# Mixer's second MLP layer with 7 block products in place of 8 for four of six pairs of token tiles

## The chip, the cores and the metric

The kernel runs on one core of a Trainium2 chip. The metric is the device time of one execution in microseconds; the time before is the median of three timed runs. The engines are TensorE (PE; its weight loads are PEld), VectorE (DVE), ScalarE (ACT), GpSimd (POOL) and SyncE (SP, which issues DMAs). Each runs its own instructions in the order of the program and waits on semaphores for the others.

## What is computed

Three stages follow each other: an attention with a delta-rule state, a mixture of experts in which one expert is chosen for each token, and a Mixer. The change lies in the Mixer's MLP (two batches of 768 tokens, 384 features, 1536 hidden):

```python
def _moe2_ref(x, w_ch1, w_ch2):
    X = np.fft.fft(np.fft.fft(x, axis=1), axis=2)
    u = x + np.real(X)
    mu = np.mean(u, axis=-1, keepdims=True)
    var = np.mean((u - mu) ** 2, axis=-1, keepdims=True)
    un = (u - mu) / np.sqrt(var + 1e-06)
    ch = np.maximum(un @ w_ch1, 0.0) @ w_ch2
    return u + ch
```

## The kernel before

The Mixer works on 12 token tiles of 128 tokens, six per batch. **Front of a batch:** sums and differences of mirrored rows (`d`, `e`, from `xa`; L1127 and L1130) are split in two fp16 parts (`zh` on ACT L1190, `zl` on DVE L1192); PE multiplies them with the tables of the Fourier transform along the tokens (`yp` L1208), ACT and DVE split the result (`Y` L1263, L1265), PE transforms along the features (`fp` L1239), and DVE makes `m` (L1251, L1252), which is added to `ur`, the tile `u` (L1127). Then the statistics of the layer norm (`bs`, `ag`, `vs`, L1282 to L1299), `un` on ACT (L1304), three transposes on PE (`up` L1320) and the two fp16 parts of the transposed tile, `uT` (L1325, L1327). The first tiles are ready before the second batch's front begins, so the MLP of the first runs between pieces of the front of the second.

**MLP.** Tiles go through in groups, `GROUPS=(2, 4, 4, 2)`. Layer 1 (`mlp1`) computes, for each of 12 blocks of 128 hidden features, nine matmuls into one PSUM tile `mp`: three slices of the features times three products of the fp16 high and low parts, the weights stationary, `uT` (256 or 512 tokens wide) moving. `relu` writes the high part `mh` (ACT) and the low part `ml` (DVE). Layer 2 (`mlp2`) takes `mh` and `ml` as the stationary operand, 128 x 128, and 384 columns of `w_ch2` as the moving one, three products per tile and block, summed over the 12 blocks in one PSUM bank per tile (`mop`). `finish` adds the bank to `ur` on DVE and sends the tile out, from SP or, for two tiles of a batch, with an indirect DMA on POOL.

**Order.** Nothing of this is in the order of the source. Each piece is a Python generator that yields what it needs (an engine for so many ns, a buffer, a flag), and `Order` plays them against a clock of its own and records each instruction when its engine is granted. `MP` holds the priority of each generator, `EB` a bias in ns between DVE and POOL for the sums and differences (`eng`, `tt`), and the resources (`h`, `o`, `mh`, `uT`) are counts of buffers. So a number in a table moves instructions on every engine. Flags hold only in this plan: on the chip an instruction waits for the semaphores of the data that it reads and writes. `n01` is the flag for the second tile of the first group, transposed.

Of the kernel before, what the change touches and what calls it, by code (L numbers as in the profile page):

```python
# [728 lines left out]
class Rest:  # L729
# [657 lines left out]
    def mlp2(s):
        nc=s.nc
        for g,m in enumerate(s.GROUPS):
            yield f"H{g}0"  # L1390
            for _ in range(m): yield ("+","o")
            pm=[s.ps.tile([128,512],F32,tag="o",name="mop",bufs=4)[:,0:384] for _ in range(m)]
            for f in range(12):
                yield f"H{g}{f}"
                hs=s.hs.pop((g,f))
                for t in range(m):
                    if t==0 or f==11: yield ("T",490*m if f<11 else 490,0)
                    for n,(a,b) in enumerate(((0,0),(1,0),(0,1))):
                        nc.tensor.matmul(out=pm[t],lhsT=hs[a][:,128*t:128*t+128],rhs=s.w_ch2(b,f),start=(f==0 and n==0),stop=(f==11 and n==2))  # L1399
                    if f==11: s.add_("F",s.finish(g,t,pm[t]))  # L1400
# [127 lines left out]
```

## Time and profile before

| | us |
|---|---|
| timed runs, median (lowest to highest) | 582.86 (581.4 to 585.84) |
| profiled execution | 580.74 |
| its span | 578.9 |
| PE busy | 470.7 |
| DVE busy | 421.7 |
| ACT busy | 322.8 |
| POOL busy | 78.9 |

The mean granted clock of TensorE over the span was 0.909. Attention takes the first 245 us, the experts 250 to 394, the Mixer the rest; the first matmul of the MLP starts at 415.60 us. The rows that are quoted below are from this execution, and their times start with its span. A start and a length are given for each instruction; since instructions on an engine overlap, a pace is read from starts. Square brackets behind a row hold the idle time ahead of it and what ended it.

### The profile page before, as it was taken

How to read it: one execution, taken by the hardware profiler on the slowest of the kernel's cores; microseconds unless marked ns; L12 is line 12 of the kernel's file. 1: busy time of each engine (PE TensorE's matmuls, PEld its weight loads, DVE VectorE, ACT ScalarE, POOL GpSimd, SP SyncE). 2: the span in 40 equal slices, each digit the busy share in tenths (PEclk: the TensorE clock that was granted, in tenths of full speed). 3: DMA queues.
4: the chain of work that ended last, by engine and by line, in shares of the span. 5: the costliest groups of instructions: out<-in, count | busy, mean ns of one | idle time of the engine just before them, and what ended most of it. 6: DMA issues, size and time to landing. Idle time of an engine off the chain costs nothing.

```text
span 578.9 us, 12899 instructions
## 1 busy us (share of the span) xinstructions
PE 470.7 (81%) x5162; PEld 375.0 (65%) x5162; DVE 421.7 (73%) x943; ACT 322.8 (56%) x729; POOL 78.9 (14%) x85
## 2 busy tenths in 40 slices
PE   0642027894689799679999999999899999999997
PEld 0531017783689698568888888788787655555575
DVE  7969989898998877469888979878987643231132
ACT  3664347898698888716766766672554332111111
POOL 6000000000000000040343332125111210000010
PEclk9965556999599789879999999999999999999999
DMA  7274125186005103839999997328100000010011
GB/s 250 50 130 121 37 49 63 63 141 156 1 3 103 29 3 100 299 99 336 388 319 316 361 305 238 118 63 274 56 1 1 28 2 0 1 55 0 1 42 41
DMA packets 66991, 67.23 MB, mean 116 GB/s; under 512 B 40086, under 2 KB 59483, under 8 KB 66928
## 3 DMA queue, kind: packets, MB, share of 16 engines
q1 hardware_dynamic: 63936, 57.59, 33.5%
q0 software_dynamic: 2992, 8.79, 4.9%
q8 instruction: 41, 0.67, 0.5%
q14 instruction: 22, 0.18, 0.1%
HBM read 51.95 MB, written 7.67 MB: 103 GB/s over the span
## 4 chain that ended last, share of the span: by engine, by line
PE 27%; issue 18%; POOL 5%; DVE 3%; DMA 1%; ACT 1%; POOLq 0%; SPq 0%; ACTq 0%; DVEq 0%
PE mp L1373 12%; PE mop L1399 12%; POOL xg L901 3%; POOL x2d L939 2%; PE fp L1239 1%; PE yp L1208 1%; DMA xa<-x2d 1%; PE up L1320 1%; DVE zl L1192 0%; DMA x2d<-ot,sim 0%; ACT zh L1190 0%; DVE e L1127 0%; DVE Y L1265 0%; DVE ws L894 0%; DVE d L1127 0%
## 5 line engine op out<-in xcount | busy, mean ns | idle before, releaser
L1383 DVE SCALAR_TENSOR_TENSOR ml<-mp,mh 128x256 f16<-128x256 f32 (+1 forms) x48 | 26.8, 558 | 81.0 <-ACT mh L1381 80.9
L1373 PE MATMUL mp<-uT,ws 128*128 128x256 f16 (+1 forms) x432 | 77.8, 326 | 0.0
L1399 PE MATMUL mop<-ws,mh 128*128 128x384 f16 x288 | 77.7, 326 | 0.0
L1381 ACT ACTIVATE mh<-mp 128x256 f16<-128x256 f32 (+1 forms) x48 | 23.5, 489 | 89.8 <-PE mp L1373 89.6
L930 PE MATMUL op<-ws,hh 128*128 128x384 f16 (+1 forms) x256 | 67.5, 326 | 0.0
L918 PE MATMUL hp<-xT,ws 128*128 128x240 f16 x576 | 64.6, 266 | 0.9 <-DVE xT L909 0.5
L312 PEld LDWEIGHTS <-KT 128*128 128x128 f16 x576 | 27.5, 118 | 51.6 <-issue 40.1
L918 PEld LDWEIGHTS <-ws 128*128 128x128 f16 x576 | 56.2, 98 | 6.9 <-issue 1.3
L1373 PEld LDWEIGHTS <-ws 128*128 128x128 f16 x432 | 42.2, 98 | 27.2
L894 DVE SCALAR_TENSOR_TENSOR ws<-raw,ws 128x1536 f16<-128x1536 f32 x32 | 55.9, 1749 | 0.0
L312 PE MATMUL ga<-ST,KT 128*128 128x64 f16 x288 | 16.2, 224 | 42.2 <-DVE ST L308 37.7
L891 ACT ACTIVATE ws<-raw 128x1536 f16<-128x1536 f32 x32 | 47.3, 1485 | 0.7 <-DMA raw<-moe_w 0.7
L1399 PE MATMUL mop<-ws,ml 128*128 128x384 f16 x144 | 46.9, 326 | 0.0
L930 PE MATMUL op<-ws,hl 128*112 128x384 f16 (+1 forms) x128 | 41.7, 326 | 0.0
L1399 PEld LDWEIGHTS <-mh 128*128 128x128 f16 x288 | 28.2, 98 | 17.8
L901 POOL DMA_INDIRECT xg<-xd,gm x16 | 23.0, 1437 | 117.4 <-DVE fl L1063 110.0
L930 PEld LDWEIGHTS <-hh 128*128 128x128 f16 (+1 forms) x256 | 29.1, 114 | 11.6
L373 DVE TENSOR_TENSOR P<-P,tmp 128x31 f32<-128x31 f32 (+15 forms) x93 | 31.5, 338 | 1.7
L371 DVE TENSOR_TENSOR tmp<-Gu,P 128x31 f32<-128x31 f32 (+15 forms) x93 | 31.2, 336 | 1.6
L921 DVE SCALAR_TENSOR_TENSOR hl<-hp,hh 128x480 f16<-128x480 f32 x32 | 20.9, 654 | 14.5 <-ACT hh L920 12.9
L939 POOL DMA_INDIRECT x2d<-ot,sim x16 | 19.3, 1204 | 86.9 <-ACT ot L935 84.4
L920 ACT ACTIVATE hh<-hp 128x480 f16<-128x480 f32 x32 | 18.1, 567 | 20.7 <-PE hp L918 19.5
(274 smaller groups left out, 1176.9 us busy)
## 6 DMA issues: line engine op xcount, KB each, us to landing
raw<-moe_w SPq DMA_DIRECT2D x64, 384.0 KB
x<-moe_w_ch SPq DMA_DIRECT2D x24, 384.0 KB
qp<-q SPq DMA_DIRECT2D x5, 512.0 KB
kp<-k SPq DMA_DIRECT2D x6, 384.0 KB
vp<-v SPq DMA_DIRECT2D x6, 384.0 KB
xd<-yb SPq DMA_DIRECT2D x48, 48.0 KB
xa<-x2d SPq DMA_DIRECT2D x6, 384.0 KB
ur<-x2d SPq DMA_DIRECT2D x2, 768.0 KB
```

The costliest lines, as they stand in the source:

```text
L312: s.nc.tensor.matmul(out=out,lhsT=st[l],rhs=mv[m],start=(first and i==0),stop=True,skip_group_check=True)
L371: nc.vector.tensor_tensor(out=x,in0=Gu[:,k,k+1:32].unsqueeze(2).to_broadcast([128,m,n]),in1=P[:,k,0:n].unsqueeze(1).to_broadcast([128,m,n] ...
L373: nc.vector.tensor_tensor(out=P[:,k+1:32,0:n],in0=P[:,k+1:32,0:n],in1=x,op=ALU.subtract)
L891: s.nc.scalar.activation(out=s.W[q][:,0].rearrange("p s c -> p (s c)"),in_=s.raw[q],func=AF.Copy,scale=WS)
L894: s.nc.vector.scalar_tensor_tensor(out=W[1],in0=s.raw[q],scalar=WS,in1=W[0],op0=ALU.mult,op1=ALU.subtract)
L901: nc.gpsimd.indirect_dma_start(out=s.xg[e][t][0:w],out_offset=None,in_=s.xd,in_offset=bass.IndirectOffsetOnAxis(ap=s.gi[0:w,8*t+e:8*t+e+1] ...
L918: nc.tensor.matmul(out=p[:,i],lhsT=s.W[q][:,a,i,128*k:128*k+128],rhs=xT[b][:,k],start=(n==0),stop=(n==8)); n+=1
L930: nc.tensor.matmul(out=s.po[t][0:w],lhsT=hs[a][:,i,128*t:128*t+w],rhs=s.W[q][:,b,i,384:768],start=(g==0 and i==0 and n==0),stop=(g==3 and ...
L939: i=s.nc.gpsimd.indirect_dma_start(out=s.x2d,out_offset=bass.IndirectOffsetOnAxis(ap=s.si[0:w,c:c+1],axis=0),in_=ot,in_offset=None,bounds_ ...
L1373: for k in range(3): nc.tensor.matmul(out=p,lhsT=s.w_ch1(a,k,f),rhs=s.uT[g][b][:,k,0:N],start=(n==0),stop=(n==8)); n+=1
L1383: nc.vector.scalar_tensor_tensor(out=hl,in0=p,scalar=0.0,in1=hh,op0=ALU.max,op1=ALU.subtract)
L1399: nc.tensor.matmul(out=pm[t],lhsT=hs[a][:,128*t:128*t+128],rhs=s.w_ch2(b,f),start=(f==0 and n==0),stop=(f==11 and n==2))
```

## The change

The groups become six pairs of tiles. For pairs 1 to 4 (`STR`), layer 2 is computed as a product of 2 x 2 blocks with seven block products (Winograd's form of Strassen's). The blocks are: two token tiles, two halves of the hidden features (block j and block j+6), two halves of the 384 output columns.

- **Layer 1** makes, for each j of 6, two `mp` of 256 tokens. For the seven products their ReLU goes to fp32 (`zz`, ACT), four 128 x 128 sums follow on DVE or POOL (`C` in `EB`), and `pair` splits three and then four of the blocks in `mh` and `ml` (ACT copy, DVE subtraction, both from SBUF).
- **Layer 2** (`seven`): for each j seven products of three matmuls with 192 columns, into four banks; `first4` and `last3` put the seven sums together, with additions on DVE or POOL.
- **The weights' sums** (`combine`): twelve sums of 128 x 2 x 192 in fp32, six ACT copies and six DVE subtractions of 128 x 2 x 384, in place in the tiles that held the raw weights (`dec`), which now stay to the end. In the plan they begin with `n01`.
- `uT` is 256 wide with three buffers; `EB` puts the second batch's sums and differences on DVE (`D1`, `S1`: -9000), and `MP` has new numbers.

```diff
-    EB={'q1': 500, 'q0': -9000, 'D1': 0, 'z0': -9000, 'S0': -9000, 'S1': -500, 'z1': 1000, 'D0': -9000}
+    EB={'T': 0, 'C': 0, 'G': 0, 'q1': 0, 'q0': -9000, 'D1': -9000, 'z0': -9000, 'S0': -9000, 'S1': -9000, 'z1': 1000, 'D0': -9000}
...
-            s.uT[g]=[s.fp.tile([128,3,512],F16,tag=f"uT{x}",name="uT",bufs=2) for x in range(2)]
+            s.uT[g]=[s.fp.tile([128,3,256],F16,tag=f"uT{x}",name="uT",bufs=3) for x in range(2)]
...
-    GROUPS=(2, 4, 4, 2)
+    GROUPS=(2, 2, 2, 2, 2, 2)
+    STR=(0, 1, 1, 1, 1, 0)
+    LASTP=(0, 0, 3, 0, 2, 1)
...
+    def combine(s):
+        nc=s.nc; A=nc.scalar; V=nc.vector
+        yield "n01"
+        for q in range(3):
+            x,y=[s.raw[32+q+3*i].rearrange("p (s c) -> p s c",s=2) for i in range(2)]
+            b11,b12,b21,b22=x[:,:,384:576],x[:,:,576:768],y[:,:,384:576],y[:,:,576:768]
+            t1,t2,t3,t4=x[:,:,0:192],x[:,:,192:384],y[:,:,0:192],y[:,:,192:384]
+            for out,i,j in ((t1,b12,b11),(t2,b22,t1),(t3,b22,b12),(t4,b21,t2)): yield from s.tt(out,i,j,ALU.subtract,"T")
+            s.TW[q]=[]
+            for z in (x,y):
+                w=z.bitcast(F16)
+                h,l=[w[:,:,768+384*i:1152+384*i] for i in range(2)]
+                yield ("A",870)
+                A.activation(out=h,in_=z[:,:,0:384],func=AF.Copy,scale=WS)
+                yield ("V",890)
+                V.scalar_tensor_tensor(out=l,in0=z[:,:,0:384],scalar=WS,in1=h,op0=ALU.mult,op1=ALU.subtract)
...
+    def relu7(s,g,j,i,p,hs):
+        nc=s.nc; z=s.zz[g,j]
+        yield ("",972+200)
+        yield ("A",264)
+        nc.scalar.activation(out=z[:,2*i:2*i+2],in_=p,func=AF.Relu)
+        yield ("-","h")
+        if i==0:
+            yield ("!",f"Z{g}{j}")
+            return
+        yield f"Z{g}{j}"
+        for n,(o,x,y,op) in enumerate(((4,0,2,ALU.add),(5,4,1,ALU.subtract),(6,1,0,ALU.subtract),(7,3,5,ALU.subtract))):
+            if n==1: s.add_("R",s.pair(g,j,0,z,hs))
+            yield from s.tt(z[:,o],z[:,x],z[:,y],op,"C",(200,470))
+        yield from s.pair(g,j,1,z,hs)
+    def pair(s,g,j,i,z,hs):
+        nc=s.nc; a,b=((0,3),(3,7))[i]
+        hh,hl=[t[:,a:b] for t in hs]
+        yield ("A",(370,475)[i])
+        nc.scalar.activation(out=hh,in_=z[:,a+1:b+1],func=AF.Copy)
+        yield ("V",(460,590)[i])
+        nc.vector.tensor_tensor(out=hl,in0=z[:,a+1:b+1],in1=hh,op=ALU.subtract)
...
+    def seven(s,g):
...
+        for j,roles in todo:
+            yield f"TW{j//2}"
+            for i in range(2): yield f"H{g}{j}{i}"
+            hs=s.hs[g,j]
+            for n,role in enumerate(roles):
...
+                p=P[role]=bank[b][:,192*c:192*c+192]
+                yield ("T",243,0)
+                for m,(x,y) in enumerate(((0,0),(1,0),(0,1))):
+                    nc.tensor.matmul(out=p,lhsT=hs[x][:,role],rhs=s.second(role,y,j),start=new and m==0,stop=True,skip_group_check=True)
+                if j==5 and n==3 and role==3: s.add_("F",s.first4(g,P))
+            if roles[-1]==6: yield ("-","mh")
+        s.add_("F",s.last3(g,bank))
...
-        o=s.o=Order(s.KEEN,s.SHARE,{"phase":s.PHASE},xa=1,z=4,Y=2,h=3,q=1,m=1,st=2,un=2,uT=2,t=1,mh=3,o=4)
+        o=s.o=Order(s.KEEN,s.SHARE,{"phase":s.PHASE},xa=1,z=4,Y=2,h=3,q=1,m=1,st=2,un=2,uT=3,t=1,mh=3,Z=2,vq=1,o=4)
...
+        if any(s.STR): s.add_("W2",s.combine())
```

How this moves instructions is shown at three places. Numbers behind a name tell its buffers apart, and each row ends with the engines that it waits for.

The first place is POOL at the start of the Mixer. The first row is the last of four gathers of `ur`, the ISA row sets up POOL for what follows. Before:

```order
L1116 DMA ur_6565<-x2d_61,mirror_3991 128x384 [waits DMASW0_49]
L1127 ISA
L1127 TENSOR_TENSOR d1_6711<-xa_6548 128x384 [waits DMAHW4_49,DVE_49]
L1127 TENSOR_TENSOR d2_6712<-xa_6548 128x384 [waits DMAHW5_49,DVE_49]
L1127 TENSOR_TENSOR e1_6875<-xa_6548 128x384 [waits DVE_49]
L1127 TENSOR_TENSOR e2_6876<-xa_6548 128x384 [waits Activation_49]
L1127 TENSOR_TENSOR e0_6874<-xa_6563 128x384 [waits DMAHW6_49,DVE_49,Activation_49]
L1127 TENSOR_TENSOR e1_6875<-e1_6875,e2_6876 128x384 [waits DVE_49]
```

After:

```order
L1116 DMA ur_6566<-x2d_61,mirror_3991 128x384 [waits DMASW0_49]
L1127 ISA
L1127 TENSOR_TENSOR dec_4922<-dec_4922 128x2x192 [waits DVE_49]
L1127 TENSOR_TENSOR dec_4922<-dec_5669,dec_4922 128x2x192 [waits Pool_49]
L1127 TENSOR_TENSOR dec_5669<-dec_5669,dec_4922 128x2x192 [waits DVE_49]
L1127 TENSOR_TENSOR dec_5669<-dec_5669,dec_4922 128x2x192 [waits Pool_49]
L1127 TENSOR_TENSOR dec_5185<-dec_5185 128x2x192
L1127 TENSOR_TENSOR dec_5929<-dec_5929,dec_5185 128x2x192 [waits DVE_49] x2
```

Behind the gathers, the first sums and differences of the second batch (`d`, `e`, which wait for the DMA of `xa`) have gone to DVE, and in their place stand the weights' sums in `dec`. The last row stands for two, of which the second is the first that reads a late result of DVE.

The second place is DVE in the front of the second batch, up to `zl` of the element that is called `e2` in both. Before:

```order
L1130 SCALAR_TENSOR_TENSOR e2_6876<-e1_6875,e0_6874 128x384 [waits Pool_49]
L1383 SCALAR_TENSOR_TENSOR ml_7082<-mp_7053,mh_7081 128x256 [waits Activation_49]
L1192 SCALAR_TENSOR_TENSOR zl_7085<-e2_6876,zh_7084 128x384 [waits Activation_49]
L1127 TENSOR_TENSOR d3_6713<-d1_6711,d2_6712 128x384
L1383 SCALAR_TENSOR_TENSOR ml_7105<-mp_7080,mh_7104 128x256 [waits Activation_49]
L1327 SCALAR_TENSOR_TENSOR uT_6921<-up_7086,uT_6920 128x3x128 [waits Activation_49]
L1192 SCALAR_TENSOR_TENSOR zl_7120<-e0_6874,zh_7119 128x384 [waits Activation_49]
L1127 TENSOR_TENSOR d1_6711<-d1_6711,d2_6712 128x384 [waits DVE_49]
```

After:

```order
L1521 SCALAR_TENSOR_TENSOR ur_6454<-mop0_6833,ur_6454 128x384 [waits PE_49]
L1439 TENSOR_TENSOR ml_7176<-zz_7177,mh_7175 128x384 [waits Activation_49]
L1378 SCALAR_TENSOR_TENSOR dec_5399<-dec_5399 128x2x384 [waits Activation_49]
L1439 TENSOR_TENSOR ml_7176<-zz_7177,mh_7175 128x512 [waits Activation_49]
L1127 TENSOR_TENSOR e1_6905<-e1_6905,e2_6906 128x384
L1378 SCALAR_TENSOR_TENSOR dec_6173<-dec_6173 128x2x384 [waits Activation_49]
L1439 TENSOR_TENSOR ml_7234<-zz_7235,mh_7233 128x384 [waits Activation_49]
L1130 SCALAR_TENSOR_TENSOR e2_6906<-e1_6905,e0_6904 128x384 [waits DVE_49]
L1127 TENSOR_TENSOR e0_6904<-e0_6904,e1_6905 128x384 [waits DVE_49]
L1192 SCALAR_TENSOR_TENSOR zl_7318<-e2_6906,zh_7317 128x384 [waits Activation_49]
```

Before, `ml` (L1383) reads PSUM between two `zl`, and the sum `e0` was POOL's. After, subtractions of `pair` (L1439, 384 or 512 wide), those of the weights (L1378) and the sums `e1` and `e0` stand ahead of `zl`.

The third place is PE in layer 2 of a group in the middle of the MLP; each matmul has a weight load of its own. Before:

```order
L1399 LDWEIGHTS mh_6841 [waits Activation_49]
L1399 MATMUL mop_6827<-ws_6244,mh_6841 128x384
L1399 LDWEIGHTS ml_6842
L1399 MATMUL mop_6827<-ws_6244,ml_6842 128x384
L1399 LDWEIGHTS mh_6841
L1399 MATMUL mop_6827<-ws_6244,mh_6841 128x384
L1399 LDWEIGHTS mh_6841
L1399 MATMUL mop_6828<-ws_6244,mh_6841 128x384
L1399 LDWEIGHTS ml_6842
L1399 MATMUL mop_6828<-ws_6244,ml_6842 128x384
```

After:

```order
L1485 LDWEIGHTS mh_7120
L1485 MATMUL mop1_7232<-ws_6198,mh_7120 128x192
L1485 LDWEIGHTS ml_7121 [waits DVE_49]
L1485 MATMUL mop1_7232<-ws_6198,ml_7121 128x192
L1485 LDWEIGHTS mh_7120
L1485 MATMUL mop1_7232<-ws_6198,mh_7120 128x192
L1485 LDWEIGHTS mh_7120
L1485 MATMUL mop1_7232<-dec_4922,mh_7120 128x192 [waits Pool_49]
L1485 LDWEIGHTS ml_7121 [waits DVE_49]
L1485 MATMUL mop1_7232<-dec_4922,ml_7121 128x192
```

One stationary block served 384 columns of one tile's bank before; now each product has 192 columns, in half a bank, and the weights come from `ws` (a block as it is) or from `dec` (a sum).

## Rows read from the trace of the kernel before

**Rows 1.** The page, part 1: engine, busy us (share of the span), instructions.
```profile
PE 470.7 (81%) x5162; PEld 375.0 (65%) x5162; DVE 421.7 (73%) x943; ACT 322.8 (56%) x729; POOL 78.9 (14%) x85
```

**Rows 2.** Windows of 10 us: busy us of each engine, granted clock, DMA.
```profile
430.00:440.00 10.00, 9.87 (x80) 7.70 (x79) 8.34 (x23) 5.28 (x14) 1.00 (x1) 1.00 0.01 2
440.00:450.00 10.00, 9.96 (x79) 7.27 (x78) 7.47 (x19) 4.33 (x12) 1.99 (x2) 1.00 0.00 0
...
500.00:510.00 10.00, 10.00 (x57) 5.44 (x55) 3.96 (x9) 1.68 (x3) 0.00 (x0) 1.00 0.01 5
```

**Rows 3.** Chain that ended last, in order of time: start us, us, what.
```profile
399.20 0.94 DVE e L1127 x2
...
457.40 3.01 PE fp L1239 x36
...
544.15 1.94 PE mp L1373 x9
546.09 1.95 PE mop L1399 x12
548.04 0.98 PE mp L1373 x9
```

**Rows 4.** Timeline of PE, 414 to 579: start us, us, what.
```profile
415.60 3.22 PE L1373 MATMUL mp<-uT,ws 128*128 128x256 f16 x27
...
453.61 0.55 PE L1320 MATMUL up<-ca,un 128*128 128x128 f32 x3 [0.63 <-ACT un L1304]
...
575.11 0.33 PE L1399 MATMUL mop<-ws,mh 128*128 128x384 f16 x1
```

**Rows 5.** Groups by form, 415 to 579, PE and PEld: count, busy, mean ns.
```profile
L1399 PE MATMUL mop<-ws,mh 128*128 128x384 f16 x288 | 77.7, 326 | 0.0
L1373 PE MATMUL mp<-uT,ws 128*128 128x512 f16 x216 | 50.5, 379 | 0.0
L1399 PE MATMUL mop<-ws,ml 128*128 128x384 f16 x144 | 46.9, 326 | 0.0
...
L1399 PEld LDWEIGHTS <-mh 128*128 128x128 f16 x288 | 28.2, 98 | 17.8
L1373 PE MATMUL mp<-uT,ws 128*128 128x256 f16 x216 | 27.3, 273 | 0.0
...
L1239 PEld LDWEIGHTS <-Y 128*128 128x128 f16 x96 | 8.3, 97 | 0.5
```

**Rows 6.** The same view, DVE and ACT.
```profile
L1383 DVE SCALAR_TENSOR_TENSOR ml<-mp,mh 128x256 f16<-128x256 f32 x24 | 10.2, 424 | 22.7 <-ACT mh L1381 22.6
...
L1381 ACT ACTIVATE mh<-mp 128x256 f16<-128x256 f32 x24 | 9.1, 381 | 26.6 <-PE mp L1373 26.4
...
L1407 DVE SCALAR_TENSOR_TENSOR ur<-mop,ur 128x384 f32<-128x384 f32 x12 | 6.0, 551 | 2.3 <-PE mop L1399 2.3
```

**Rows 7.** Timeline of POOL, 394 to 437.
```profile
396.06 0.94 POOL L1116 DMA_INDIRECT ur<-x2d,mirror  x1 [0.30 <-issue]
403.13 2.26 POOL L1127 TENSOR_TENSOR d<-xa 128x384 f32<-128x384 f32 x2 [6.12 <-DMA xa<-x2d]
...
428.66 1.00 POOL L1127 TENSOR_TENSOR e<-e,e 128x384 f32<-128x384 f32 x1 [6.65 <-DVE e L1127]
```

**Rows 8.** Timeline of DVE, 394 to 437.
```profile
399.12 1.02 DVE L1127 TENSOR_TENSOR e<-xa 128x384 f32<-128x384 f32 x2
400.06 1.08 DVE L1265 TENSOR_TENSOR Y<-yp,Y 128x256 f16<-128x256 f32 x3
...
403.81 0.72 DVE L1192 SCALAR_TENSOR_TENSOR zl<-e,zh 128x384 f16<-128x384 f32 x1 [0.59 <-ACT zh L1190]
...
405.10 0.70 DVE L1127 TENSOR_TENSOR ur<-ur,m 128x384 f32<-128x384 f32 x1
...
407.98 0.16 DVE L1291 RECIPROCAL vs<-vs 128x1 f32<-128x1 f32 x1 [0.20 <-ACT vs L1289]
...
429.15 0.93 DVE L1127 TENSOR_TENSOR ur<-ur,m 128x384 f32<-128x384 f32 x1
```

More of the change, by code (lines that the diff above doesn't have):

```diff
@@ new lines, in pair, with bank @@
+    def pair(s,g,j,i,z,hs):
[5 more added lines that the diff above has]
+        nc.vector.tensor_tensor(out=hl,in0=z[:,a+1:b+1],in1=hh,op=ALU.subtract)
+        s.hs[g,j]=hs
+        yield ("!",f"H{g}{j}{i}")
+        if i:
+            yield f"H{g}{j}0"
+            yield ("-","Z")
+    def bank(s,i): return s.ps.tile([128,512],F32,tag="o",name=f"mop{i}",bufs=4)[:,0:384]
@@ L1387, in mlp2 @@
     def mlp2(s):
         nc=s.nc
[L1389 to L1400, printed above, removed]
-                yield ("-","mh")
+        for g in range(6):
+            if s.STR[g]:
+                yield from s.seven(g); continue
+            yield f"H{g}00"
+            for _ in range(2): yield ("+","o")
+            pm=[s.bank(0) for _ in range(2)]
+            for j in range(6):
+                for i in range(2): yield f"H{g}{j}{i}"
+                hs=s.hs.pop((g,j))
+                for t in range(2):
+                    if t==0 or j==5: yield ("T",1920 if j<5 else 960,0)
+                    for i in range(2):
+                        for n,(x,y) in enumerate(((0,0),(1,0),(0,1))):
+                            nc.tensor.matmul(out=pm[t],lhsT=hs[x][:,2*i+t],rhs=s.w_ch2(y,j+6*i),start=(j==0 and i==0 and n==0),stop=(j==5 and i==1 and n==2))
+                    if j==5: s.add_("F",s.finish(g,t,pm[t]))
+                yield ("-","mh")
@@ new lines, in seven @@
+    def seven(s,g):
+        nc=s.nc
+        yield f"H{g}00"
+        bank={}
+        L=s.LASTP[g]
+        P={}
+        todo=[(j,s.ROLES) for j in range(6-L)]+[(j,s.ROLES[:4]) for j in range(6-L,6)]+[(j,s.ROLES[4:]) for j in range(6-L,6)]
+        for j,roles in todo:
+            yield f"TW{j//2}"
+            for i in range(2): yield f"H{g}{j}{i}"
+            hs=s.hs[g,j]
+            for n,role in enumerate(roles):
+                b,c=s.PLACE[role]
+                new=b not in bank
+                if new:
+                    yield ("+","o")
+                    bank[b]=s.bank(1)
+                p=P[role]=bank[b][:,192*c:192*c+192]
[5 more added lines that the diff above has]
+        s.add_("F",s.last3(g,bank))
@@ new lines, with rows, first4 @@
+    PLACE={0:(0,0),4:(0,1),5:(1,0),1:(2,0),3:(2,1),2:(3,0),6:(3,1)}
+    def rows(s,g,t):
+        b,k=divmod(2*g+t,6); k=s.TILES[k]
+        return b,k,s.ur[b][:,k]
+    def first4(s,g,P):
+        nc=s.nc; V=nc.vector; c=1/US/WS/WS
+        v=s.fq.tile([128,2,192],F32,tag="vq",name="vq",bufs=1); w=s.fq.tile([128,192],F32,tag="wq",name="wq",bufs=1)
+        u1,u2=s.rows(g,1)[2],s.rows(g,0)[2]
+        yield ("",450)
+        yield ("+","vq")
+        yield ("A",220)
+        nc.scalar.activation(out=v[:,0],in_=P[0],func=AF.Copy,scale=c)
+        yield ("V",270)
+        V.scalar_tensor_tensor(out=w,in0=P[4],scalar=c,in1=v[:,0],op0=ALU.mult,op1=ALU.add)
+        yield ("-","o")
+        yield ("V",270)
+        V.scalar_tensor_tensor(out=v[:,1],in0=P[3],scalar=c,in1=w,op0=ALU.mult,op1=ALU.add)
+        yield ("V",270)
+        V.scalar_tensor_tensor(out=w,in0=P[5],scalar=c,in1=w,op0=ALU.mult,op1=ALU.add)
+        yield ("-","o")
+        yield from s.tt(u2.rearrange("p (s c) -> p s c",s=2),u2.rearrange("p (s c) -> p s c",s=2),w.unsqueeze(1).to_broadcast([128,2,192]),ALU.add,"G",(480,1150))
+        yield from s.tt(u1,u1,v.rearrange("p s c -> p (s c)"),ALU.add,"G",(480,1150))
+        yield ("-","vq")
+        yield ("!",f"f{g}")
@@ L1402, in finish, with last3 @@
+    def last3(s,g,bank):
+        yield f"f{g}"
+        for t,b in ((0,2),(1,3)): s.add_("F",s.finish(g,t,bank[b]))
     def finish(s,g,t,p):
         nc=s.nc
-        b,k=divmod(sum(s.GROUPS[:g])+t,6); k=s.TILES[k]; u=s.ur[b][:,k]
-        yield ("",700)
+        b,k,u=s.rows(g,t)
+        yield ("",450)
         yield ("V",469)
```

62 lines of the change are left out of this document (37 added, 25 removed).

## The prediction

> **What bounds the kernel now.** I read the page first: TensorE (PE) is the busiest engine, 470.7 us of a 578.9 us span [rows 1]. That share is an average over three stages, so the next view is the table of 10 us windows over the Mixer's MLP: PE is busy 9.87, 9.96 and 10.00 us of 10 at a granted clock of 1.00 (the upper level, 2.4 GHz), while VectorE (DVE) falls from 8.34 to 3.96 and ScalarE (ACT) from 5.28 to 1.68 [rows 2]. The chain of work that ended last says the same: from the first `mp` to the last `mop` it is PE after PE, then DVE's last additions and an output DMA [rows 3]. So in this stage the end is set by the sum of PE's matmul time. Ahead of it, at 396 to 406 us, the chain runs through DVE: `e` on DVE at 399.20 is a piece of it [rows 3]. There DVE's delay moves the first `mp` (415.60, [rows 4]), and with it everything behind. These two stretches decide.
>
> **PE's sum.** Back-to-back paces, from starts: twelve 384-column matmuls take 1.95 us, 162.5 ns each; nine of 512 columns 1.94 us, 215.6 ns; nine of 256 columns 0.98 us, 108.9 ns [rows 3]. The change adds a width that this stage does not have, 192. The nearest row is L1239's `fp` with 194 columns: 36 of them take 3.01 us, 83.6 ns each [rows 3]; scaled to 192, 82.7 ns.
> Layer 2 has 432 matmuls of 384 columns (288 on `mh`, 144 on `ml`) and layer 1 has 216 of 512 and 216 of 256 [rows 5]. After, four of the six pairs use 7 products: 4 pairs x 6 chunks x 7 products x 3 hi/lo terms = 504 matmuls of 192 columns, and two pairs keep 2 x 72 = 144 of 384. Layer 1 is 6 x 12 x 9 = 648 of 256.
> Removed: 288 x 0.1625 = 46.8 and 216 x 0.2156 = 46.6, together 93.4 us. Added: 504 x 0.0827 = 41.7 and 432 x 0.1089 = 47.0, together 88.7 us. **PE: -4.65 us.** The seven products alone save 5.1; narrower layer 1 gives 0.5 back.
>
> **Are 192-column matmuls really that short?** Each has its own weight load, and the load records of `mop` last 98 ns [rows 5], longer than 82.7. If a load could not hide under the matmul before it, each matmul would cost 98 ns. But L1239's matmuls have a load each too (97 ns, [rows 5]) and take 83.6 ns each [rows 3]; the loads overlap each other or the record holds waiting. I take 82.7; the upper bound is 98 (+7.7 us over the 504).
> By the Trainium skill, "TensorE: Matmul & The Clock Gate", section "LDWEIGHTS (loading the stationary operand)", a 128-column load takes about 128/1.2 = 107 ns; if that set the pace, the 504 would cost an estimated 12.2 us more and the change would lose. By that rule the `fp` matmuls would take 107 ns as well, and the trace has 83.6 [rows 3].
>
> **The vector engines in steady state.** One chunk of a 7-product pair is 18 x 0.109 + 21 x 0.0827 = 3.70 us of PE. DVE then has no `ml` from PSUM but two subtractions (384 and 512 elements wide) and part of four 128-wide sums; POOL takes the other sums. A 256-wide `ml` took 0.42 us and the 384-wide `finish` 0.55 [rows 6]; one of 512 is bounded by those of 384 and twice 256, 0.55 to 0.85. A 128-wide one has bounds 0.16 (the width-1 `vs`, [rows 8]) and 0.42. So DVE has 1.1 to 1.4 us for the subtractions and at most 1.7 for the sums: 3.1 of 3.70, under PE. ACT has two 256-wide ReLUs (0.38 each, [rows 6]) and two copies of at most 0.76: 2.3. Neither is the bound on average.
> The weights' sums (twelve adds, six ACT copies, six DVE subtractions of 768 elements) come once; on DVE the six are at most 6 x 1.1 = 6.6 us, twice the 384-wide price; and the nine adds of the second batch that POOL did before go to DVE. They fall in the 30 us in which DVE had 8.34 and 7.47 of 10 us busy [rows 2], the tight place. The order shown ahead (DVE, second batch) puts `zl_7318` behind eight pieces of layer 2's work; walking PE's and DVE's orders with the paces above, it comes about 0.3 us ahead of the `yp` that wants it, and one chunk's `ml` in the next pair about 0.7 us late for its product. With a small wait for a PSUM bank I put **new PE stalls at +0.8 us**, bounds 0 and 2. PE's stalls here were small before, 0.63 us at 453.61 the longest [rows 4].
>
> **The front: what POOL does early.** The weights' sums are held by the planner until the second tile is transposed (`n01`), but this sets only their place in each engine's order. Their first instructions on POOL stand directly behind the four gathers of `ur`, and the waits printed in the order are for DVE (the scaled weights, written in the MoE stage) and POOL itself; the seventh waits for a late DVE result. Before, POOL's next work there was `d1` and `d2`, which waited for a DMA. The trace shows the gap: the last gather ends at 397.00 and POOL's next sum starts at 403.13 [rows 7]. The new sums have 2 x 192 = 384 elements, the size of `d` or `e`, which takes POOL 1.00 us [rows 7]. So six of them can run from 397 to 403, in the stretch where DVE is the chain.
> That collides. DVE operations with two SBUF inputs stretch when a POOL sum runs: `ur<-ur,m` at 429.15 took 0.93 us where two `e` in a row took 1.02 together and the 384-wide `finish` 0.55, and ended 0.42 us behind POOL's 428.66 + 1.00; `zl` at 403.81 took 0.72 and `ur` at 405.10 0.70 beside POOL's two sums of 403.13 to 405.39 [rows 6 to 8]. Between 397 and 404 DVE has about nine such operations (`d`, `zl`, `e`, [rows 8]). Bounds: below, DVE always goes first, nothing lost, and the 0.3 us now lost to POOL's two sums (0.72 and 0.70 against 0.55) comes back, -0.3. Above, POOL's 6.0 us are exclusive except while DVE reads PSUM (three `Y`, 1.08 us) or waits for ACT's `zh` (0.59, twice; [rows 8]): 6.0 - 2.3 - 0.3 = +3.4. The nearest row is 429.15, 0.38 us lost to one POOL sum: 6 x 0.38 - 0.3 = **+2.0 us**, which I take.
> The Trainium skill, "SBUF — State Buffer", section "Who interferes with whom", says that the port pair which DVE needs for a second SBUF input is shared with GpSimd under an exclusive lock; rows 7 and 8 agree, 0.93 us in place of 0.55.
>
> **Sum.** -4.65 + 0.8 + 2.0 = -1.85 us on the profiled execution's 580.74 us: 578.9. The median of the timed runs of before is 582.86, 2.1 above that execution; carried over, **581.0 us**. The tail is the same (the last pair has no 7 products). Own range of this case: -4.65 + 0 - 0.3 to -4.65 + 2 + 3.4, that is 577.9 to 583.6.
>
> **Rivals.**
> - *All hidden.* DVE wins against POOL in front, and the reordering also removes PE's stalls of some 1.6 us (0.63 of them in one row): -4.65 - 1.6 = -6.25, 576.6. For it: the 0.63 us is a wait for ACT's `un`, front work that the new order sets elsewhere; against: the stretched operations of [rows 8]. Chance 0.12.
> - *POOL starts late.* Two POOL configuration records stand behind the gathers, and the trace does not show how long POOL is kept by them; if until about 403 (the next start, [rows 7]), the sums meet DVE at 403 to 409, where few of its operations have two SBUF inputs: two to three times 0.38, about +1. -4.65 + 0.8 + 1.0 = -2.85, 580.0. Chance 0.17.
> - *Loads set the pace.* 98 ns per 192-column matmul: -4.65 + 7.7 = +3.05, and with no other term 585.9. Against it: 83.6 ns. Chance 0.06.
> - *DVE becomes the bound, slower.* In the first two 7-product pairs DVE also has the weights' sums and the second batch. If each of the 24 subtractions there (both inputs in SBUF) meets a POOL sum, 24 x 0.38 = 9.1 us are lost where DVE has little spare, and PE waits in order: -4.65 + 2.0 + 9.1 = +6.5, 589.4. It decides from the point where DVE falls behind by more than the 0.3 us of `zl_7318`. Chance 0.08.
> - *No gain at all*, the front's upper bound and both stalls: +0.75, inside the forecast's own range.
> The forecast has the remaining 0.57.
>
> **How the numbers follow.** About 1% is what a measurement of this kernel can tell from no change: 577.0 and 588.7. The all-hidden case lies just beyond the first: faster 0.12. Of the others only the DVE-bound case passes the second: slower 0.08. Within 1%: 0.80. The range 576.5 to 586.0 holds all cases but the last, with what the bounds let spill over.
>
> **What would show it.** Right: L1485's matmuls start every 83 ns; the first `mp` near 417.6 in place of 415.60; POOL's first `dec` sum at 397 with DVE's `zl`, `d` and `e` beside it at 0.7 to 0.9 us; from the first `mp` to the last matmul about 155.8 us in place of 159.7. Wrong: a `dec` sum that starts at 403 or later; `zl` and `e` at 0.55 beside POOL; 98 ns per product; PE idle rows behind DVE `ml` or `zl` that add up to several us; a longer tail.

## The result and the profile after

The changed kernel took 589.11 us (median of 7 runs), beside 584.66 us for the kernel before in the same comparison, 4.5 us more by medians. The ratio on record is 1.0093, 95% interval 1.0072 to 1.0113, which is 5.4 us slower (4.2 to 6.6), where 1.85 us faster was forecast; 589.11 lies outside the range of 576.5 to 586.0.

The profiled execution of after took 590.29 us, span 588.3. Its page, part 1 (engine, busy us, share of the span, instructions), against [rows 1]:

```profile
PE 470.9 (80%) x5598; PEld 411.6 (70%) x5598; DVE 475.3 (81%) x1065; ACT 356.1 (61%) x811; POOL 101.1 (17%) x121
```

PE is as busy as before, with 436 matmuls more; DVE has 54 us more (421.7 to 475.3) and ACT 33. The windows of 10 us, columns as in [rows 2]:

```profile
400.00:410.00 10.00, 7.00 (x58) 5.48 (x56) 9.38 (x12) 2.19 (x5) 6.99 (x6) 0.83 0.63 217
...
450.00:460.00 10.00, 10.00 (x91) 8.38 (x90) 9.65 (x16) 5.25 (x11) 6.52 (x9) 1.00 0.11 41
460.00:470.00 10.00, 8.24 (x84) 7.01 (x82) 8.46 (x17) 4.68 (x12) 4.36 (x7) 1.00 0.00 0
...
500.00:510.00 10.00, 9.54 (x104) 8.92 (x102) 7.86 (x24) 7.09 (x17) 0.75 (x1) 1.00 0.00 0
550.00:560.00 10.00, 8.30 (x87) 7.64 (x86) 6.93 (x24) 6.11 (x14) 0.00 (x0) 1.00 0.00 0
```

Before, no window from 460 to 570 had PE below 10.00; now PE idles 1.8 us in 460 to 470 behind a window with DVE at 9.65, and 1.7 us in 550 to 560; DVE has 7.86 us of work from 500 to 510, where it had 3.96. The timeline of PE has the first `mp`, a transpose that waited, and the last matmul (it answers [rows 4]):

```profile
422.57 6.17 PE L1405 MATMUL mp<-uT,ws 128*128 128x256 f16 x54
...
553.15 0.55 PE L1320 MATMUL up<-ca,un 128*128 128x128 f32 x3 [1.70 <-ACT un L1304]
...
584.52 0.33 PE L1461 MATMUL mop<-ws,mh 128*128 128x384 f16 x1
```

The difference of the two profiled executions, 9.4 us of span, divides so. The end of the last weight scaling is that of DVE's last `ws`, in the first row before and in the second after:

```profile
388.28 5.09 DVE L894 SCALAR_TENSOR_TENSOR ws<-dec,ws 128x1536 f16<-128x1536 f32 x3
...
391.02 5.09 DVE L894 SCALAR_TENSOR_TENSOR ws<-dec,ws 128x1536 f16<-128x1536 f32 x3
```

The last matmul is taken to end 0.16 us, its pace, behind its start.

| stretch | before | after | difference |
|---|---|---|---|
| start of the span to the end of the last weight scaling (`ws` on DVE) | 393.37 | 396.11 | +2.7 |
| from there to the first `mp` | 22.23 | 26.47 | +4.2 |
| first `mp` to the end of the last matmul | 159.67 | 162.11 | +2.4 |
| from there to the end | 3.63 | 3.62 | 0.0 |

The first line is not the change's: in the kernels below, whose first two stages are the same, that end lies between 393.5 and 396.6 us; in e12_front6, which up to there is the kernel before, it is at 395.97. The profiled execution of before is at the low end of its kernel's times, that of after at the high end of its seven. The second and third line are what is to be explained; their 6.6 us, from one execution each, are at the upper end of what the timed runs give. In the MLP, PE's own sum is what was forecast: 159.7 less 1.6 of stalls less 4.65 is 153.4 us, and the starts of after, less the pace of the matmul ahead of each, leave 8.6 us of stalls in 162.1, which is 153.5 us of work. So the change did save PE 4.6 us, as forecast, and new stalls of 7 us took them.

### The profile page after: what moved, and what is told of

Same layout as the page of the kernel before. It is cut to its first block, busy times and chain, and to the rows that moved or that the text cites. A ratio compares the mean times of both kernels' runs of the same rounds, so it can differ in the third digit from the quotient of the medians.

```text
span 588.3 us, 14017 instructions
## 1 busy us (share of the span) xinstructions
PE 470.9 (80%) x5598; PEld 411.6 (70%) x5598; DVE 475.3 (81%) x1065; ACT 356.1 (61%) x811; POOL 101.1 (17%) x121
## 4 chain that ended last, share of the span: by engine, by line
PE 21%; issue 15%; DVE 10%; POOL 7%; ACT 4%; DMA 0%; POOLq 0%; DVEq 0%; ACTq 0%
PE mp L1405 9%; PE mop L1485 4%; PE mop L1461 3%; POOL xg L901 3%; POOL x2d L939 2%; DVE ws L894 1%; ACT mh L1437 1%; PE hp L918 1%; DVE ml L1439 1%; POOL zz L1127 1%; PE fp L1239 1%; PE op L930 1%; DVE e L1127 1%; DVE zl L1192 1%; PE up L1320 1%
## 5 line engine op out<-in xcount | busy, mean ns | idle before, releaser
L1405 PE MATMUL mp<-uT,ws 128*128 128x256 f16 x648 | 77.4, 273 | 0.0
L1405 PEld LDWEIGHTS <-ws 128*128 128x128 f16 x648 | 62.9, 98 | 7.4
L918 PEld LDWEIGHTS <-ws 128*128 128x128 f16 x576 | 56.2, 98 | 6.9 <-issue 1.2
L1439 DVE TENSOR_TENSOR ml<-zz,mh 128x384 f16<-128x384 f32 (+1 forms) x48 | 31.0, 646 | 13.1 <-ACT mh L1437 12.8
L1437 ACT ACTIVATE mh<-zz 128x384 f16<-128x384 f32 (+1 forms) x48 | 27.2, 574 | 19.1 <-POOL zz L1127 9.6
L1127 POOL TENSOR_TENSOR zz<-zz 128x128 f32<-128x128 f32 x38 | 22.4, 601 | 65.1 <-ACT zz L1423 46.4
L1485 PEld LDWEIGHTS <-mh 128*128 128x128 f16 x336 | 30.9, 98 | 0.8 <-ACT mh L1437 0.2
L1423 ACT ACTIVATE zz<-mp 128x256 f32<-128x256 f32 x48 | 17.9, 378 | 21.5 <-PE mp L1405 20.9
```

Source lines behind the costliest of these rows:

```text
L918: nc.tensor.matmul(out=p[:,i],lhsT=s.W[q][:,a,i,128*k:128*k+128],rhs=xT[b][:,k],start=(n==0),stop=(n==8)); n+=1
L1405: for k in range(3): nc.tensor.matmul(out=p,lhsT=s.w_ch1(x,k,j+6*i),rhs=s.uT[g][y][:,k],start=(n==0),stop=(n==8)); n+=1
L1437: nc.scalar.activation(out=hh,in_=z[:,a+1:b+1],func=AF.Copy)
L1439: nc.vector.tensor_tensor(out=hl,in0=z[:,a+1:b+1],in1=hh,op=ALU.subtract)
L1485: nc.tensor.matmul(out=p,lhsT=hs[x][:,role],rhs=s.second(role,y,j),start=new and m==0,stop=True,skip_group_check=True)
```

## What the trace of after shows

**Front.** Timeline of POOL and of DVE where the weights' sums run; they answer [rows 7, 8]:

```profile
398.65 0.95 POOL L1116 DMA_INDIRECT ur<-x2d,mirror  x1 [0.31 <-issue]
399.72 7.35 POOL L1127 TENSOR_TENSOR dec<-dec 128x384 f32<-128x384 f32 x6
...
399.14 2.00 DVE L1127 TENSOR_TENSOR d<-xa 128x384 f32<-128x384 f32 x1 [0.42 <-issue]
401.07 1.34 DVE L1192 SCALAR_TENSOR_TENSOR zl<-d,zh 128x384 f16<-128x384 f32 x1
402.33 1.35 DVE L1130 SCALAR_TENSOR_TENSOR d<-d,d 128x384 f32<-128x384 f32 x1
404.27 0.68 DVE L1192 SCALAR_TENSOR_TENSOR zl<-d,zh 128x384 f16<-128x384 f32 x1 [0.59 <-ACT zh L1190]
404.87 2.61 DVE L1127 TENSOR_TENSOR e<-xa 128x384 f32<-128x384 f32 x2
407.40 1.07 DVE L1265 TENSOR_TENSOR Y<-yp,Y 128x256 f16<-128x256 f32 x3
```

Before, the same operations of DVE stood so ([rows 8] has the two `e`):

```profile
396.56 0.56 DVE L1127 TENSOR_TENSOR d<-xa 128x384 f32<-128x384 f32 x1 [0.45 <-DMA xa<-x2d]
397.04 0.55 DVE L1192 SCALAR_TENSOR_TENSOR zl<-d,zh 128x384 f16<-128x384 f32 x1
397.51 0.55 DVE L1130 SCALAR_TENSOR_TENSOR d<-d,d 128x384 f32<-128x384 f32 x1
398.64 0.56 DVE L1192 SCALAR_TENSOR_TENSOR zl<-d,zh 128x384 f16<-128x384 f32 x1 [0.59 <-ACT zh L1190]
```

The sums begin right behind the last gather, and take 7.35 us for six. DVE's `d`, `zl`, `d`, `zl` and two `e` take 2.00, 1.34, 1.35, 0.68 and 2.61 us where before they took 0.56, 0.55, 0.55, 0.56 and 1.02: 4.7 us lost. The two engines take turns: all of these operations but the second `zl` lose some 0.8 us or more, beside sums of 1.0 to 1.3. (The first `d` starts 0.57 us ahead of the first sum and still ends 0.43 us behind its end; why it did not have its turn first is not shown.) `Y`, which reads PSUM, has its 1.07.

**MLP.** The pace, from the chain of work (start us, us, what), against [rows 3]:

```profile
519.94 1.73 PE mop L1485 x21
```

21 matmuls of 192 columns in 1.73 us are 82.4 ns each, with a weight load each; 82.7 was forecast. What PE waited for between 420 and 579 us (engine line, waited for, us in total, times, longest):

```profile
PE up L1320 <- ACT un L1304: 4.0, 5, 1.7
PE fp L1239 <- DVE Y L1265: 0.7, 2, 0.4
PE yp L1208 <- ACT zh L1190: 0.6, 1, 0.6
PE yp L1208 <- DVE zl L1192: 0.5, 1, 0.5
PE mop L1485 <- DVE ml L1439: 0.5, 1, 0.5
```

Two of the places show how they arise. The chain from 489 to 497 us:

```profile
489.71 0.48 DVE ur L1521
...
490.21 1.87 DMA out_dram<-ur
...
492.89 0.99 POOL out_dram L1529
...
493.92 0.88 POOL zz L1127 x2
...
494.82 0.64 ACT mh L1437
...
495.49 0.70 DVE ml L1439
...
496.24 0.34 PE mop L1485 x2
```

A finished tile goes out by SP; POOL's indirect output DMA waits until that has landed, and two sums (`zz`), a copy (`mh`), a subtraction (`ml`) and PE's product stand in line behind it on four engines. The second is around 546 us, on POOL, ACT and DVE:

```profile
546.00 0.98 POOL L1529 DMA_INDIRECT out_dram<-ur,mirror  x1 [2.83 <-DVE ur L1127]
547.01 0.47 POOL L1127 TENSOR_TENSOR zz<-zz 128x128 f32<-128x128 f32 x1
...
547.51 0.63 ACT L1437 ACTIVATE mh<-zz 128x512 f16<-128x512 f32 x1 [3.77 <-POOL zz L1127]
...
545.23 0.56 DVE L1127 TENSOR_TENSOR ur<-ur,m 128x384 f32<-128x384 f32 x1
548.17 0.69 DVE L1439 TENSOR_TENSOR ml<-zz,mh 128x512 f16<-128x512 f32 x1 [2.39 <-ACT mh L1437]
548.78 0.55 DVE L1282 BATCH_NORM_STATS2 bs<-ur 128x6 f32<-128x384 f32 x1
```

The statistics `bs` need `ur`, which is written by 545.79. They start at 548.78, behind `ml` in DVE's order, which waits for `mh`, for `zz`, for the output DMA. The DMA's own row names DVE's `ur` as what it waited for last; but SP's output DMA ahead of it is issued at 543.35 us, and POOL's starts 2.65 us behind that, as the one in the chain above starts 2.68 us behind its own (490.21 to 492.89). So this is read as the same wait. From there the layer norm takes until 553.15, when PE has idled 1.70 us for the transpose of `un`. So a late output DMA on POOL becomes a late layer norm.

## The experiments

The numbers of the traces first; "front" is from the end of the last weight scaling to the first `mp`, "MLP" from there to the end of the last matmul (153.4 would be PE without a stall where four pairs have 7 products). Both are from one profiled execution of each kernel; the MLP of before and of e12_front6, where it is the same program, is 159.67 in both. Ratios are to the kernel before on the same chip.

| kernel | ratio, 95% interval | front us | MLP us |
|---|---|---|---|
| before | 1 | 22.23 | 159.67 |
| after | 1.0093, 1.0072 to 1.0113 | 26.47 | 162.11 |
| e1_gate | 1.0062, 1.0035 to 1.0089 | 21.79 | 163.49 |
| e2_thin | 0.9991, 0.9967 to 1.0014 | 21.40 | 158.52 |
| e3_late | 1.0007, 0.9983 to 1.0030 | 21.61 | 160.79 |
| e4_pairs | 1.0125, 1.0082 to 1.0168 | 21.40 | 168.45 |
| e5_zzdve | 1.0006, 0.9988 to 1.0025 | 21.66 | 160.92 |
| e6_sumdve | 0.9977, 0.9952 to 1.0002 | 21.40 | 159.89 |
| e7_two | 1.0185, 1.0143 to 1.0227 | 21.71 | 170.68 |
| e8_alldve | 0.9998, 0.9975 to 1.0021 | 21.69 | 160.35 |
| e9_up800 | 1.0048, 1.0027 to 1.0069 | 21.81 | 163.81 |
| e9_up1600 | 1.0060, 1.0031 to 1.0088 | 21.42 | 163.15 |
| e9_up_yp | 1.0095, 1.0066 to 1.0123 | 21.70 | 164.86 |
| e10_thin | 0.9916, 0.9894 to 0.9937 | 21.77 | 157.19 |
| e11_thin12 | 0.9959, 0.9939 to 0.9978 | 21.67 | 157.34 |
| e12_front6 | 1.0076, 1.0051 to 1.0100 | 26.90 | 159.67 |

**The front: the sums held back, and the meeting alone.** e1_gate puts a small POOL copy ahead of the sums:

```diff
         yield "n01"
+        gt=s.fp.tile([128,1],F32,name="gt")
+        nc.gpsimd.tensor_copy(out=gt,in_=s.uT[0][1][:,0,128:129])
```

> The changed kernel with one small POOL copy ahead of the weights' sums that reads the second tile's transposed values, so that the sums really begin with that tile (before the copy they began at 399.72 us, behind the gathers). Theory A, POOL's early sums hold up DVE in the front: the stretch from the ur gathers' end to the first layer 1 matmul gets 4 to 4.5 us shorter, the sums start near 420 and the whole is about 4 us faster than the changed kernel, unless they now hold DVE up later. Rival B, the front was late for another reason (a later start of the stage, another order): the first layer 1 matmul stays some 26 us behind the end of the last weight scaling, and the time does not move by more than 1 us.

e12_front6 is the kernel before with six sums that nobody reads, behind the gathers:

```diff
         o.add(s.arrive(f"ur{b}",4000))
+        if b:
+            sc=s.fp.tile([128,2,384],F32,name="sc")
+            nc.gpsimd.memset(sc,0.0)
+            for i in range(6): nc.gpsimd.tensor_tensor(out=sc[:,0],in0=sc[:,0],in1=sc[:,1],op=ALU.subtract)
```

> The kernel before, with a memset and six 128 x 384 sums on POOL on a scratch tile of their own behind the gathers of ur; nothing reads them. Theory A, the meeting of POOL's sums with DVE's two-input operations is the whole loss in front: the first layer 1 matmul comes 4 to 5 us later (26 to 27 us behind the last weight scaling, 22.2 before), the MLP behind it is unchanged, the time 4 to 5 us longer. Rival, the loss in the changed kernel came with its data (the weights' tiles, in which DVE and POOL both work): within 1 us of the kernel before.

With the gate the front is 4.7 us shorter (26.47 to 21.79) and the ratio falls from 1.0093 to 1.0062; 1.4 us of it goes into one new stall in the MLP, since the sums now meet DVE behind 416 us. Timelines of POOL, DVE and PE of e1_gate:

```profile
416.39 6.39 POOL L1127 TENSOR_TENSOR dec<-dec 128x384 f32<-128x384 f32 x6
...
416.65 1.15 DVE L1127 TENSOR_TENSOR ur<-ur,m 128x384 f32<-128x384 f32 x1
417.72 1.34 DVE L1127 TENSOR_TENSOR e<-e,e 128x384 f32<-128x384 f32 x1
...
416.02 2.13 PE L1407 MATMUL mp<-uT,ws 128*128 128x256 f16 x18
419.45 1.80 PE L1407 MATMUL mp<-uT,ws 128*128 128x256 f16 x15 [1.30 <-DVE ml L1417]
```

`ur` and `e` take 1.15 and 1.34 us, an `ml` behind them is late, and PE waits 1.30 us for its PSUM buffer (1.46 us from start to start, less the pace). In e12_front6, timelines of POOL and DVE:

```profile
400.17 7.88 POOL L1121 TENSOR_TENSOR sc<-sc 128x384 f32<-128x384 f32 x6
...
401.84 2.62 DVE L1131 TENSOR_TENSOR e<-xa 128x384 f32<-128x384 f32 x2
404.38 1.07 DVE L1269 TENSOR_TENSOR Y<-yp,Y 128x256 f16<-128x256 f32 x3
405.38 1.82 DVE L1131 TENSOR_TENSOR e<-e,e 128x384 f32<-128x384 f32 x2
407.12 1.34 DVE L1196 SCALAR_TENSOR_TENSOR zl<-e,zh 128x384 f16<-128x384 f32 x1
```

The front is 26.90 us and the MLP 159.67 as before: 4.7 us, about the 0.8% of the ratio, from sums on a tile of their own. So the data of the weights is not needed for it, and DVE has no wait for POOL's data in this stretch. Both rivals fell, theory A stands. (POOL's own two `d`, which met DVE at 403 us before, come behind the sums here, from 408.01 us, and meet it there; their part is within the 4.7.) Here too `e` twice takes 2.62 us and 1.82, `zl` 1.34, and `Y` from PSUM its 1.07.

**The output DMAs.** e3_late, on top of the gate:

```diff
-            nc.gpsimd.indirect_dma_start(out=s.O["y"],...)
+            s.hold=getattr(s,"hold",[])+[(b,k,u)]
+        if g>=4:
+            for b,k,u in getattr(s,"hold",[]): nc.gpsimd.indirect_dma_start(out=s.O["y"],...)
+            s.hold=[]
```

> The gated kernel with POOL's four indirect output DMAs issued only behind the last 7-product pair, when POOL has no more sums. Theory E, an output DMA on POOL that waits for SP's output DMAs holds the sums behind it (the one at 492.89 us stands 2.5 us in the chain): the stalls at 494 to 496 and at 553 go, 2 to 3 us of the 8.4, and the time falls by as much. Rival: they are not on the path often enough, under 1 us; or the DMAs at the end make the tail longer, up to 2 us.

The MLP is 2.7 us shorter than with the gate (163.49 to 160.79), as the upper end of the expectation has it, and the tail is not longer. The first of the four, in POOL's timeline of e3_late:

```profile
560.71 1.01 POOL L1533 DMA_INDIRECT out_dram<-ur,mirror  x1 [19.42 <-DMA out_dram<-ur]
```

It starts when POOL has no sums left. PE's waits (415 to 580 us) list 2.6 us for `un`, where e1_gate as after had 4.0:

```profile
PE up L1320 <- ACT un L1304: 2.6, 5, 1.1
```

**The sums of the 7-product pairs: their time, and their engine.** e2_thin, on top of the gate, with one column per sum:

```diff
-            yield from s.tt(z[:,o],z[:,x],z[:,y],op,"C",(200,470))
+            c=lambda v: z[:,0,v-4:v-3] if v>3 else z[:,v,4:5]
+            yield from s.tt(c(o),c(x),c(y),op,"C",(200,470))
...
-        nc.scalar.activation(out=hh,in_=z[:,a+1:b+1],func=AF.Copy)
+        nc.scalar.activation(out=hh,in_=z[:,(a+1)%4:(a+1)%4+b-a],func=AF.Copy)
```

> The same, and each of the four 128 x 128 sums per chunk is made of one column only (the rest of these sums is left out), with every instruction, its engine and its place kept. Theory C, the sums' time on POOL and DVE, and the port between them, make PE's new stalls of about 8.4 us in the MLP: stalls fall to 2 to 3 us and the time falls by about 5 us against the gated kernel. Rival D, the stalls come from the longer chain of engines (ReLU, sum, copy, subtraction) and from what stands in line on ACT and DVE: stalls stay above 6 us.

The MLP goes from 163.49 to 158.52, 5.0 us, as theory C has it. But its stalls fall from 10.1 to 5.1 us, which is neither the 2 to 3 of theory C nor the more than 6 of rival D: the sums' time is about half of them, and the other half is left when it is gone. e5_zzdve and e8_alldve then ask whether it is POOL's slowness and its meeting with DVE (on top of e3_late; `"C"` are these sums, `"T"` the weights'; e8 has no gate):

```diff
         e,c=s.eng(*c,s.EB.get(x,0))
         yield c
+        if x=="C": e=s.nc.vector      # e5_zzdve
+        if x=="T": e=s.nc.vector      # e6_sumdve, no gate
+        if x in "CT": e=s.nc.vector   # e8_alldve, no gate
```

> The kernel with the sums gated and the output DMAs late, and all 128 x 128 sums of the 7-product pairs issued on DVE in the recorded order (38 of 96 were on POOL). Theory C1, POOL is the trouble (a sum there takes 0.45 to 1.0 us against 0.29, and locks DVE out): PE's stalls fall from about 8 to 5 us and the time by 2 to 3 us. Rival, DVE's own load is the trouble in the first of these pairs: 38 x 0.2 = 8 us more on DVE make the stalls at 456 to 462 longer, and the time the same or up to 3 us worse.

> The kernel with the output DMAs late and without the gate; all twelve weights' sums are on DVE in the recorded place (nine were on POOL). The front is free of POOL, first layer 1 matmul some 21.5 us behind the last weight scaling as in the gated kernel. If the gated kernel's 1.46 us stall at 419 comes from POOL's sums holding DVE's ml, it goes, but nine sums of 0.47 us are added to DVE between 416 and 446: within 2 us of the late kernel, either way. If DVE is saturated there, stalls rise by 2 to 4 us.

> Late output DMAs, no gate; all weights' sums and all 128 x 128 sums on DVE in the recorded order, so that POOL does nothing beside DVE but the ur additions of first4. No time is lost at the port; DVE has some 12 us more work than in the gated kernel. If the port and POOL's slow sums are the larger part, stalls are 5 us or less and the time is 3 us under the late kernel's; if DVE's load is, it is 2 us or more above.

All three are within 1 us of e3_late in the MLP: 160.92, 159.89, 160.35. C1 fell in this part: PE's stalls stay where they were. DVE is busy 9.89 us from 450 to 460 in e5_zzdve and 9.18 in e3_late, so the time that no longer is lost to POOL seems to be spent by DVE itself. Putting the weights' sums on DVE took the stall at 419 from 1.46 to 0.89 us (start to start, less the pace). e6_sumdve is the best complete version, 0.9977 of the kernel before with an interval of 0.9952 to 1.0002: a gain over the changed kernel of 1.2%, and over the kernel before none that this resolves.

**Where the sums hurt.** On top of e6_sumdve, thin sums in all four pairs, and in the first two alone (the condition `g<3` in the lines of e2_thin):

> The kernel with the weights' sums on DVE and the output DMAs late, and the four 128 x 128 sums of each chunk of one column only in all 7-product pairs (the rest of these sums is left out), every instruction in its place. If the causes add, the MLP stretch is the 159.9 us of the full version less the sums' share, 155 to 156 us (PE's own sum is 153.4), and the time 3.5 to 5 us below it. If the output DMAs and the sums were the same stall counted twice, the stretch stays above 157.5.

> The same with the thin sums in the first two 7-product pairs alone, which run beside the second batch's front. If that is where DVE is short of time, this has nearly all of the gain of the kernel with all sums thin; if the sums cost the same everywhere, half of it.

157.19 and 157.34 us: in these two executions nearly all of the 2.7 us that thin sums give is in the first two pairs, beside the second batch's front. The timed runs do not say the same. Full sums have 0.9977, thin ones in the first two pairs 0.9959 and in all four 0.9916, and the last two intervals do not meet: by these values, the first two pairs have less than half of the gain. The profiled execution of e11_thin12 was the fastest of its ten, that of e10_thin the slowest of its four. So it is shown that the sums cost time; where they cost it is not settled.

The first expectation, 155 to 156, was too low by 1.2 for the stretch, though the time is 3.6 us less by the ratios, as it had it. In the traces the sums' share with late DMAs is 2.7 us, where it was 5.0 with the DMAs in place (and with the weights' sums on POOL), so the two are partly one stall. In e11_thin12 PE is busy 10.00 us of 10 in both windows from 450 to 470 with DVE at 9.17 and 9.36: a DVE as busy as that does not by itself make PE wait. What PE still waits for there:

```profile
PE up L1321 <- ACT un L1305: 1.8, 5, 0.4
PE mp L1406 <- DVE ml L1416: 0.7, 1, 0.7
```

**PE's place in line.** On top of e6_sumdve, the plan asks for transposes later (`e9_up_yp` also for `yp` of the second batch, by 900 ns):

```diff
+        if g: yield ("",1600)   # e9_up800: 800
         yield ("T",255)
         for j in range(3): nc.tensor.transpose(...)
```

> The kernel with the weights' sums on DVE and the output DMAs late; in the plan each transposed tile after the first pair is asked for 800 ns later, so that PE's queue has matmuls of the MLP ahead of the transposes. PE's stalls ahead of up were 4.6 us in five places. If they come from PE standing in line behind a layer norm that is 0.5 to 1.2 us later than planned, they fall to under 2 us and the time by 2 to 3 us, below the kernel before. If the lateness grows with the delay (the layer norm itself waits for the MLP's work on ACT and DVE), they stay above 3 us.

> The same with 1600 ns. PE in line behind the layer norm: stalls ahead of up under 1 us, unless the pairs' layer 1 then waits for its tile; time 3 to 4 us below the kernel with sums on DVE. The other theory: no better than with 800 ns.

> 1600 ns ahead of the transposes and 900 ns ahead of the second batch's products along the sequence (yp). The 1.5 us of stalls at 456 to 463, ahead of yp and fp, go too if they are a late zl in PE's line: some 1.5 us better than with the transposes alone. If DVE is saturated there, they move and stay.

All are slower, by 3.3 to 5.0 us of MLP. The waits of e9_up1600:

```profile
PE up L1322 <- ACT un L1305: 1.5, 2, 0.9
PE fp L1240 <- DVE Y L1266: 1.4, 1, 1.4
PE yp L1209 <- DVE zl L1193: 1.1, 1, 1.1
```

The wait for `un` falls to 1.5 us in two places, but 1.4 us for `Y` and 1.1 for `zl` come in its stead, and the profile lists six smaller ones. That fits a lateness in the vector engines, of which PE's order only decides where it is met. It is not shown: these kernels also have a new plan, which is a second cause that they don't separate.

**The tables.** e4_pairs has no 7 products (`STR` all 0), e7_two only those of pairs 3 and 4 (on top of e3_late):

> The changed kernel's grouping in six pairs and its tables, but no 7 products and no weights' sums: 8 products in all pairs. PE's sum is 0.5 us above the kernel before (216 matmuls of 512 columns become 432 of 256). If the regrouping and the new tables are harmless, it is within 1 us of the kernel before, about +0.5; if they cause the stalls (layer norm chain of the second batch late), it is 3 us or more slower than before.

> Gated and late, with 7 products only in the pairs 3 and 4 (STR two of six), the plan made anew with the same tables. PE's sum is then about 2 us below the kernel before (half of -5.1, and +0.5). If the stalls come from the work on DVE, ACT and POOL that the first two such pairs add beside the second batch's front, stalls fall below 5 us and the time is under the late kernel's. If they come from the tables, made for another plan, stalls stay at 8 or rise and the time is 2 to 5 us above the late kernel's.

Both are the slowest of all. Most of e4's loss, 7.4 of the 8.8 us in the MLP, is at one wait and right behind it:

```profile
PE up L1320 <- ACT un L1304: 5.4, 3, 4.5
```

4.5 us for the `un` of the last tiles at 558 us; in e7 the longest is 5.9. Behind the wait 2.7 us more are lost in e4: a wait of 0.6 us for `uT`, and matmuls at a slower pace, for behind the idle time the granted clock was 0.50, the lower level (1.2 GHz), from 558 to 561 us and 0.74 from 561 to 565. It may be that the priorities, made for a plan in which DVE and ACT are full, set the second batch's front too late in another; no run shows it. So these two say nothing on grouping or on the share of each pair: a test that lets the planner run anew measures the tables with it. What the new tables, or the sums and differences that went to DVE with `D1` and `S1`, cost in the changed kernel itself stays untested.

## Why the prediction was wrong

- **PE's sum: right.** -4.65 us forecast, which is 153.4 us of work; 153.5 measured, with 82.4 ns for 192 columns. The rival in which loads set the pace fell. The Trainium skill, "TensorE: Matmul & The Clock Gate", section "LDWEIGHTS (loading the stationary operand)", has about 107 ns for a load of 128 columns; as a floor for back-to-back matmuls with a load each, the 82.4 ns do not bear it out.
- **The front: mechanism right, size wrong.** +2.0 us was taken between -0.3 and +3.4; 4.2 to 4.7 were measured (after, e1_gate, e12_front6). The step that failed is the price from one row, 0.38 us lost per POOL sum: it came from an operation that started 0.49 us into a sum of 1.00. In a run of sums the engines alternate and each DVE operation loses about a whole one, 0.8 us in `zl` and `d`, 1.4 in the first `d`. The bound failed too, since it had POOL's sum at 1.00 us; between DVE's operations six took 7.35. The -0.3 us in the sum was right in its sign: without POOL's sums the front is 21.4 to 21.8 us, 0.4 to 0.8 below before.
- **New PE stalls: this step failed most.** +0.8 us was put, with bounds 0 and 2; 7.0 more than before were measured. The walk through two orders with the rows' durations had left out that ACT and POOL stand in line too. Runs put 2.7 us of it on POOL's output DMAs (e3_late), which the prediction did not price at all, and some 2.6 us on the time of the 128 x 128 sums (e10_thin, e11_thin12). The gate had put in 1.4 us of its own, of which the weights' sums on DVE took 0.9 back (e6_sumdve). With all of these gone, 157.34 us against a sum of 153.4 leave 2.3 us more than the 1.6 of before, as waits for `un` and for one `ml`; that rest was not taken apart further, and its cause stays open.
- **The rivals.** "DVE becomes the bound" was the one to weigh higher than 0.08: windows at 9.65 of 10 and the missing 0.3 us of `zl` came true. That its 589.4 us is close to the 589.11 measured is luck: it was priced by 9.1 us of meetings with POOL's sums in the first two pairs, and with those sums on DVE the MLP is within 0.5 us of what it was (e5_zzdve, e8_alldve).
- **The chances.** The change of 0.93% is within the 1% that was called no change at 0.80, but it went the other way than the forecast, and the range ended 3 us too low. Of the 8.1 us between 581.0 and 589.11, 1.8 are not the change's: the kernel before had 582.86 when the forecast was made and 584.66 in the comparison. On the older base the changed kernel would still be outside the range, at 588.3 (582.86 x 1.0093).

## What to carry to other kernels

When products are saved on a bound engine by giving sums to engines that are not, count their queues, not their busy shares: the sums stand in line with what feeds the bound engine elsewhere, and one late DMA in that line is paid by all behind it. Look where each moved instruction can start on the chip, since a flag in a plan is no wait: here sums that the plan had behind the second transposed tile (416 us with the gate) ran at 400, beside the one stretch in which DVE set the pace. And price an engine pair that shares a port by whole operations in turn, not by one overlap.

## What the runs showed of the hardware

POOL sums and DVE operations with two SBUF inputs alternate, on the weights' tiles and on a scratch tile alike: six sums of 128 x 384 on a scratch tile made the front 4.7 us longer (e12_front6), and took 7.88 us themselves, where one alone takes 1.00 us [rows 7]. The Trainium skill, "SBUF — State Buffer", section "Who interferes with whom", states an exclusive lock between the two engines. The runs agree, and show in these runs of sums that the turn passes to the other engine after nearly every operation. With PE idle 3.0 us of the window from 400 to 410 us, the granted clock was 0.83 there, so part of it was at the lower level (1.2 GHz); it is 1.00 in the windows behind. In e4_pairs it was 0.50 from 558 to 561 us, behind 4.5 us of idle PE, so that a long stall there cost more than its own length.
